# Attention backward on one core: loads of a head pair in one piece, taken in turn with the group's, and a tail that finishes each tile one step later

## The chip, the cores and the metric

The kernel runs on one core of a Trainium2 chip. A time is the device time of one execution in microseconds (us), and less is better. A core has five engines that run side by side and wait for each other by semaphores: TensorE (PE in the profile), VectorE (DVE), ScalarE (ACT), GpSimd (POOL) and SyncE (SP), which here does nothing but issue DMAs. Each engine takes its instructions strictly in the order of the program, and so a DMA that SP or POOL issues goes out only when everything ahead of it on that engine has gone out.

## The reference, cut to what matters

The kernel computes a transformer block, attention and a gated feed-forward side by side on one layer norm, and all its gradients:

```
xn  = layernorm(x)                          # x: 2048 rows of 448
out = x + attention(xn, wqkv, wo) + (silu(xn @ w_gate) * (xn @ w_up)) @ w_down
returns out and the gradients of x, wqkv, wo, w_gate, w_up, w_down for grad_out
```

Attention has 16 heads of 28 columns (padded to 32) over 2048 positions. With P = softmax(q k' / sqrt(28)) the backward pass needs dV = P' dO, dS = P * (dO V' - delta), dQ = dS K and dK = dS' Q. The gradient of x is the layer norm's backward of the sum of what comes back through wqkv, w_gate and w_up, plus grad_out.

## The kernel before, in words

The work has four stages, one after the other.

**Prologue and stage A** (0 to 657 us). Layer norm, the projection of q, k and v, attention forward, and the feed-forward with its weight gradients. Heads are taken in 4 groups of 4; a group's q, k and v, transposed, are tiles of 128 partitions (4 heads by 32) by 2048 positions. `proj_done` (L198) has POOL write them to DRAM (`vT_d`, `qT_d`, `kT_d`, one store each, L204 to L206), and `o_items` has POOL write the transposed gradient of the attention output there in four quarters (`dOT_d`, L525).

**Stage B** (657 to 1471 us), attention backward, lines 826 to 918. Heads go by pairs: 8 pairs, two to a group. A pair's work is 64 units, one for each 512 keys (kc), half of the queries (w) and 128 queries (qi), 512 units in all. In a unit PE forms the scores (L852) and dO V' (L863), both as products over 32 rows: the tile named qT holds q' of the two heads in its rows 0 to 63 and dO' in rows 64 to 127, and the tile named kT holds k' and v' likewise. ACT takes the exponential (L870), DVE multiplies to dS (tile `ds`, L881, 8 buffers), PE accumulates dV and dK from both (L749). dQ needs dS transposed: of 8 units two are transposed by PE (L776) and six by a DMA transpose that SP issues (`dsT`, L883). I call 8 units a **window** and number it W, 0 to 63. Beside this, a window has PE do one "job" of plain matrix products: a tile of rows of the output, of the gradient through the feed-forward, or a part of the wqkv gradient (L672 to L734). What a job needs (`ck`, 448 or 576 KB) SP loads two windows ahead (`job_load`, L655).

SP's order is written out by hand. In a window it issues at position 0 the job's load, at position 4 the loads of operands for what is to come, and at each of six units the transpose of `ds`; also every second window the transpose of a finished dK/dV block (`dkv_sp`, L762), and in the first two windows of a pair that of the last pair's dQ (`dq_sp`, L818). The loads to come wait in three lists: `pload` (the next pair's qT and kT), `gload` (the next group's row-major q, k, dO: `v_sp`, `vT`, `O_sp`) and `wload` (weights). `load_pair` (L546) makes the pair's loads from four DRAM tensors, since two of them go to rows 0 to 63 and two to rows 64 to 127; cut in two along the positions this gives 8 DMAs of 64 partitions by 1024 columns, 128 KB each. `load_group` (L558) makes 6 DMAs of 128 partitions by 1024 columns, 256 KB each. At position 4 up to two of `pload`, one of `gload` and two of `wload` are issued (L844):

```
for lst, n in ((pload, 2), (gload, 1), (wload, 2)):
    for f in lst[:n]:
        f()
    del lst[:n]
```

A pair's loads are so issued in the first four windows of the pair before it, and a group's in the first six windows of the group before it.

**Between** (1471 to 1494 us): the last part of the wqkv gradient.

**The tail** (1494 to 1548 us), lines 950 to 981: the gradient of x, 16 tiles of 128 rows. For a tile PE sums 14 products into PSUM (L957, L959); ACT copies it with a row sum s1 (`g_sb`, L963); DVE multiplies it by xn with a row sum s2 (`junk`, L966) and makes two numbers per row of s1 and s2 (`bb` L970, `cc` L972); ACT scales (`t1`, L975, which needs `bb`); DVE adds (`t2`, L977, which needs `t1` and `cc`); POOL adds grad_out (`dx`, L980); SP stores (L981). PSUM has 3 buffers for the tiles, the small tiles 3 each.

Of the kernel before, what the change touches and what calls it, by code (L numbers as in the profile page):

```python
# [10 lines left out]
ALU = mybir.AluOpType  # L11
# [26 lines left out]
def kernel(  # L38
# [27 lines left out]
    qT_d = dram.tile([G, P, S], BF16, name="qT_d")  # L66
    kT_d = dram.tile([G, P, S], BF16, name="kT_d")
    vT_d = dram.tile([G, P, S], BF16, name="vT_d")
    dOT_d = dram.tile([G, P, S], BF16, name="dOT_d")
# [128 lines left out]
    def proj_done(g):  # L198

        qT, kT, vT = (qk_tiles[(g, i)] for i in range(3))  # L200
        if g > 0:
            v = v_tiles[g] = qkp.tile([P, NT, P], BF16, name="v_sp")
            sp.dma_start_transpose(out=v[:], in_=vT[:])
        pool.dma_start(out=vT_d[g], in_=vT[:])  # L204
        pool.dma_start(out=qT_d[g], in_=qT[:])
        pool.dma_start(out=kT_d[g], in_=kT[:])  # L206
# [260 lines left out]
    def o_items(g, qc, o_ps):  # L467
# [29 lines left out]
        def do(i):  # L497
# [27 lines left out]
            pool.dma_start(out=dOT_d[g, :, qc * 512:(qc + 1) * 512], in_=dT[:])  # L525
# [20 lines left out]
    def load_pair(pr, parts):  # L546

        g, r = pr // 2, 64 * (pr % 2)
        q = qkp.tile([P, S], BF16, name="qT")
        k = qkp.tile([P, S], BF16, name="kT")  # L550
        qd[pr] = (q, k)
        n = S // parts
        return [lambda i=i, dst=dst, r0=r0, src=src: sp.dma_start(
                    out=dst[r0:r0 + 64, i:i + n], in_=src[g, r:r + 64, i:i + n])
                for r0, srcs in ((0, (qT_d, kT_d)), (64, (dOT_d, vT_d)))
                for dst, src in zip((q, k), srcs) for i in range(0, S, n)]
# [274 lines left out]
    for k in range(N + 2 * UW):  # L831
        W, pos = k // UW, k % UW
        if k < N:
# [7 lines left out]
            if pos == 4:  # L841
                if W == len(jobs) - 1:
                    wload.extend(load_w("wq", 2))
                for lst, n in ((pload, 2), (gload, 1), (wload, 2)):  # L844
                    for f in lst[:n]:
                        f()
                    del lst[:n]
# [74 lines left out]
    with ExitStack() as fin:  # L922
# [26 lines left out]
        wq = wtile["wq"]  # L949
        for t in range(NT):  # L950
# [7 lines left out]
            for n in range(3 * G):  # L958
# [17 lines left out]
            t2 = wk.tile([P, D], FP32, name="t2")  # L976
            dve.scalar_tensor_tensor(out=t2[:], in0=xn_sp[:, t, :D], scalar=cc[:, 0:1], in1=t1[:],  # L977
                                     op0=ALU.mult, op1=ALU.add)
            dx = wk.tile([P, D], BF16, name="dx")
            pool.tensor_tensor(out=dx[:], in0=t2[:], in1=dy_t[:, t, :], op=ALU.add)  # L980
            sp.dma_start(out=out1_d[:, t, :], in_=dx[:])  # L981
# [31 lines left out]
```

## Time and profile before

| | |
|---|---|
| time, median of 3 runs | 1550.76 us (1550.44 to 1550.81) |
| the profiled execution's own time | 1549.43 us |
| its span (first to last instruction) | 1547.7 us |
| PE, ACT, DVE, POOL busy over the span | 91%, 77%, 71%, 26% |
| stage A, 50 to 657 us | PE busy 573.2 of 607.0 us, DMA share 0.78 |
| stage B, 657 to 1471 us | PE busy 744.2 of 814.0 us, DMA share 1.07 |
| tail, 1494.3 to 1547.7 us | PE busy 43.0 of 53.4 us |

A line of the profile names the line of the kernel, the engine, the operation, and the tiles it writes and reads (out<-in). In a list in order of time the first two numbers are the start and the duration in us; "x3" means that three are merged into one line, and what stands in brackets is the idle time before them and what ended it. SPq and ACTq are the issuing of DMAs by SP and ACT. A table by stretches gives, for each stretch, its length and the busy time of each engine, then PEclk, the clock that TensorE was granted as a share of full speed, then the mean share of time that the 16 DMA engines were busy (packets that overlap count twice, so it can pass 1), and GB/s.

### The profile page before, as it was taken

The page shows a single profiled execution, that of the slowest core. Times are in us where ns is not written, and L with a number is a line of the kernel's source. Part 1 is how long each engine was busy: PE and PEld are TensorE (multiplying, and loading weights), DVE is VectorE, ACT ScalarE, POOL GpSimd, SP SyncE. Part 2 cuts the span into 40 slices and gives each one's busy share as a digit, 9 for nine tenths or more (in the row PEclk, how much of TensorE's full clock was granted, in tenths as well). Part 3 has the DMA queues.
Part 4 walks back from the last instruction along what each step waited for, and adds up shares of the span by engine and source line. Part 5 has one row for each costly group of instructions (what it writes and reads, how often), then busy time and mean ns, then how long its engine had stood idle before and what let it go on. Part 6 is the DMA issues. An engine that isn't in the chain of part 4 may idle for free.

```text
span 1547.7 us, 32024 instructions
## 1 busy us (share of the span) xinstructions
PE 1412.8 (91%) x12176; PEld 597.7 (39%) x12176; DVE 1099.4 (71%) x1421; ACT 1187.9 (77%) x1333; POOL 396.1 (26%) x664
## 2 busy tenths in 40 slices
PE   6899999999999989988988988989999889999987
PEld 3333333333333333433433444433335333543353
DVE  7654555656666657476877877878878789888935
ACT  6898988888788878676767867878778778888724
POOL 4341433343435355310110111111102101111033
PEclk9999999999999999999999999999999999999999
DMA  9985758767978689799999999999999999999994
GB/s 225 189 174 113 157 101 173 161 142 141 179 154 164 148 173 215 159 205 200 214 204 206 196 199 205 198 200 198 207 197 197 200 192 197 174 192 215 188 274 142
DMA packets 682106, 285.12 MB, mean 184 GB/s; under 512 B 637136, under 2 KB 650464, under 8 KB 681952
## 3 DMA queue, kind: packets, MB, share of 16 engines
q1 hardware_dynamic: 652016, 210.03, 74.6%
q0 software_dynamic: 25968, 64.53, 16.8%
q10 hardware_dynamic: 3968, 8.52, 1.6%
q8 instruction: 95, 1.56, 0.4%
q14 instruction: 59, 0.48, 0.1%
HBM read 67.34 MB, written 63.44 MB: 85 GB/s over the span
## 4 chain that ended last, share of the span: by engine, by line
PE 56%; DMA 13%; ACT 13%; DVE 8%; issue 6%; SPq 1%; POOL 1%; ACTq 0%; DVEq 0%; POOLq 0%
DMA dsT<-ds 9%; PE f_ps L357 7%; PE sd L852 6%; PE s_ps L600 6%; PE f_ps L383 6%; ACT E L870 5%; PE aux L719 4%; PE acc L749 4%; PE aux L796 4%; PE aux L776 4%; PE o_ps L582 4%; ACT eT L605 4%; DVE ds L881 3%; ACT dsT L783 3%; PE aux L713 3%
## 5 line engine op out<-in xcount | busy, mean ns | idle before, releaser
L881 DVE TENSOR_TENSOR ds<-sd,E 128x1024 bf16<-128x1024 f32 x512 | 611.4, 1220 | 137.5 <-DMA dsT<-ds 52.6
L870 ACT ACTIVATE E<-sd 128x1024 bf16<-128x1024 f32 x512 | 516.9, 1024 | 178.4 <-PE sd L863 140.2
L605 ACT ACTIVATE eT<-s_ps 128x1024 bf16<-128x1024 f32 x512 | 495.8, 1026 | 93.1 <-PE s_ps L600 89.6
L852 PE MATMUL sd<-kT,qT 32*128 32x512 bf16 x1024 | 201.8, 390 | 24.7 <-DVE ds L881 22.3
L863 PE MATMUL sd<-kT,qT 32*128 32x512 bf16 x1024 | 202.6, 389 | 23.6 <-ACT E L870 22.7
L749 PE MATMUL acc<-ds,v_sp 128*32 128x512 bf16 x1024 | 204.6, 395 | 0.7 <-DVE ds L881 0.7
L749 PE MATMUL acc<-E,O_sp 128*32 128x512 bf16 x1024 | 204.3, 395 | 0.2 <-ACT dkv_o L755 0.2
L600 PE MATMUL s_ps<-qT,kT 32*128 32x512 bf16 x1024 | 148.0, 386 | 7.8 <-ACT eT L605 5.6
L422 POOL DMA_DIRECT2D hd_d<-fT x168 | 126.9, 769 | 15.5 <-DVE fT L407 6.8
L383 PE MATMUL f_ps<-xnT,wgu 128*128 128x512 bf16 x448 | 118.8, 383 | 4.9 <-DVE w_sb L409 4.7
L764 POOL DMA_DIRECT2D dqkv_d<-dkv_o x64 | 39.3, 619 | 289.1 <-ACT dkv_o L755 287.3
L719 PE MATMUL aux<-W,ck 128*128 128x448 bf16 x448 | 108.4, 359 | 3.4
L852 PEld LDWEIGHTS <-qT 32*128 32x128 bf16 x1024 | 51.3, 91 | 154.1 <-issue 145.5
L582 PE MATMUL o_ps<-eT,v_sp 128*32 128x512 bf16 x1024 | 103.4, 394 | 0.6
L357 PE MATMUL f_ps<-xn_sp,f_sp 128*128 128x448 bf16 x448 | 99.1, 354 | 0.0
L749 PEld LDWEIGHTS <-O_sp 128*32 128x32 bf16 x1024 | 50.4, 94 | 113.4 <-issue 103.4
L600 PEld LDWEIGHTS <-kT 32*128 32x128 bf16 x1024 | 40.7, 91 | 137.7 <-issue 132.7
L776 PE MATMUL aux<-ident_bf,ds 128*128 128x128 bf16 x1024 | 79.4, 221 | 11.2 <-DVE dq_acc L808 5.8
L863 PEld LDWEIGHTS <-qT 32*128 32x128 bf16 x1024 | 65.4, 91 | 62.1 <-issue 58.2
L357 PEld LDWEIGHTS <-f_sp 128*128 128x128 bf16 x672 | 58.2, 98 | 77.4 <-issue 23.4
L776 PEld LDWEIGHTS <-ds 128*128 128x128 bf16 x1024 | 61.8, 98 | 39.8 <-issue 39.4
L395 DVE SCALAR_TENSOR_TENSOR g<-t_sb,f_ps 128x512 f32<-128x512 f32 x56 | 38.4, 686 | 53.3 <-ACT t_sb L393 53.2
(133 smaller groups left out, 1766.5 us busy)
## 6 DMA issues: line engine op xcount, KB each, us to landing
hd_d<-fT POOLq DMA_DIRECT2D x168, 128.0 KB, 4.4
ck<-hd_d SPq DMA_DIRECT2D x32, 448.0 KB, 4.4
ck<-hd_d SPq DMA_DIRECT2D x16, 576.0 KB, 5.1
dsT<-ds SPq DMA_TRANSPOSE x384, 4.2
dqkv_d<-dkv_o POOLq DMA_DIRECT2D x64, 64.0 KB, 3.8
dq_c<-dqkv_d ACTq DMA_DIRECT2D x5, 768.0 KB, 6.5
W<-wT_d SPq DMA_DIRECT2D x14, 224.0 KB, 3.6
out_dram<-dw_o POOLq DMA_DIRECT2D x28, 96.0 KB, 4.0
```

The source lines that it names most:

```text
L357: pe.matmul(acc[:, :D], lhsT=src[:, 12 * (t // 4) + 4 * wi + t % 4, :], rhs=rhs[:, t, :D], start=(t == 0), stop=(t == NT - 1))
L383: pe.matmul(st[name][:], lhsT=w(c), rhs=src[:, tsl, c, :], start=(c == 0), stop=(c == 3))
L582: pe.matmul(o_ps[HP * hh:HP * (hh + 1), :], lhsT=v[:, kt, HP * hh:HP * (hh + 1)], rhs=e[hh // 2][:, hh % 2, :], start=(kt == 0), stop=(kt ...
L600: pe.matmul(s_ps[:, j, :], lhsT=kT[r:r + HP, kt * P:(kt + 1) * P], rhs=qT[r:r + HP, qc * 512:(qc + 1) * 512], start=True, stop=True, tile_ ...
L605: act.activation(out=e[:], in_=s_ps[:], func=ACT.Exp, scale=SCALE)
L719: return [lambda n=n: pe.matmul(ps[:, :D], lhsT=t[:, n, :], rhs=w[:, n, :], start=(n == 0), stop=(n == NFC - 1)) for n in range(NFC)]
L749: pe.matmul(acc[r:r + HP, :], lhsT=src[:, qt, 64 * hp + HP * j:64 * hp + HP * j + HP], rhs=m[:, j, :], start=(qt == 0), stop=(qt == NT - 1 ...
L776: pe.transpose(ps[:, i, :], ds[:, i // 4, (i % 4) * P:(i % 4 + 1) * P], ident_bf[:])
L852: pe.matmul(s_ps[:, j, :], lhsT=q[HP * j:HP * j + HP, qt * P:(qt + 1) * P], rhs=kv[HP * j:HP * j + HP, kc * 512:(kc + 1) * 512], start=Tru ...
L863: pe.matmul(d_ps[:, j, :], lhsT=q[r:r + HP, qt * P:(qt + 1) * P], rhs=kv[r:r + HP, kc * 512:(kc + 1) * 512], start=True, stop=True, tile_p ...
L870: act.activation(out=E[k][:], in_=s_ps[:], func=ACT.Exp, scale=SCALE)
L881: dve.tensor_tensor(out=DS[k - 1][:], in0=d_ps[:], in1=E[k - 1][:], op=ALU.mult)
```

## The change

Three things are changed.

1. **One tensor for each operand of a pair.** `qT_d` and `dOT_d` become `qdo_d`, and `kT_d` and `vT_d` become `kv_d`: a slab for each pair whose rows 0 to 63 and 64 to 127 are what the pair's tile holds. `load_pair` loads a whole tile of 128 partitions at a time, so a pair has 4 loads of 256 KB instead of 8 of 128 KB, ordered first halves first. In exchange POOL's stores are cut by head pair: six of 64 partitions for three of 128 in `proj_done`, two for one in `o_items`.
2. **One load in a window.** In a window with an even number one piece of `pload` is issued, in one with an odd number one of `gload`; `wload` stays at two. A pair's four loads go out in windows 0, 2, 4 and 6 of the pair before, a group's six in windows 1, 3, 5, 7, 9 and 11 of the group before.
3. **The tail in two steps.** `t2`, `dx` and the store of tile t are issued after `bb` and `cc` of tile t+1, and `dx` of the last three tiles is made by DVE instead of POOL.

```diff
-    qT_d = dram.tile([G, P, S], BF16, name="qT_d")
-    kT_d = dram.tile([G, P, S], BF16, name="kT_d")
-    vT_d = dram.tile([G, P, S], BF16, name="vT_d")
-    dOT_d = dram.tile([G, P, S], BF16, name="dOT_d")
+    qdo_d = dram.tile([2 * G, P, S], BF16, name="qdo_d")
+    kv_d = dram.tile([2 * G, P, S], BF16, name="kv_d")
...
-        pool.dma_start(out=vT_d[g], in_=vT[:])
-        pool.dma_start(out=qT_d[g], in_=qT[:])
-        pool.dma_start(out=kT_d[g], in_=kT[:])
+        for hp in range(2):
+            rows = slice(64 * hp, 64 * hp + 64)
+            for dst, src in ((kv_d[2 * g + hp, 64:], vT), (qdo_d[2 * g + hp, :64], qT), (kv_d[2 * g + hp, :64], kT)):
+                pool.dma_start(out=dst, in_=src[rows, :])
...
-            pool.dma_start(out=dOT_d[g, :, qc * 512:(qc + 1) * 512], in_=dT[:])
+            for hp in range(2):
+                pool.dma_start(out=qdo_d[2 * g + hp, 64:, qc * 512:(qc + 1) * 512],
+                               in_=dT[64 * hp:64 * hp + 64, :])
...
-        g, r = pr // 2, 64 * (pr % 2)
...
-        return [lambda i=i, dst=dst, r0=r0, src=src: sp.dma_start(
-                    out=dst[r0:r0 + 64, i:i + n], in_=src[g, r:r + 64, i:i + n])
-                for r0, srcs in ((0, (qT_d, kT_d)), (64, (dOT_d, vT_d)))
-                for dst, src in zip((q, k), srcs) for i in range(0, S, n)]
+        return [lambda i=i, dst=dst, src=src: sp.dma_start(out=dst[:, i:i + n], in_=src[pr, :, i:i + n])
+                for i in range(0, S, n) for dst, src in ((q, qdo_d), (k, kv_d))]
...
-                for lst, n in ((pload, 2), (gload, 1), (wload, 2)):
+                for lst, n in ((pload, 1 - W % 2), (gload, W % 2), (wload, 2)):
...
+        def finish(t, t1, cc):
+            t2 = wk.tile([P, D], FP32, name="t2")
+            dve.scalar_tensor_tensor(out=t2[:], in0=xn_sp[:, t, :D], scalar=cc[:, 0:1], in1=t1[:],
+                                     op0=ALU.mult, op1=ALU.add)
+            dx = wk.tile([P, D], BF16, name="dx")
+            add = pool if t < NT - 3 else dve
+            add.tensor_tensor(out=dx[:], in0=t2[:], in1=dy_t[:, t, :], op=ALU.add)
+            sp.dma_start(out=out1_d[:, t, :], in_=dx[:])
+
         for t in range(NT):
...
             act.activation(out=t1[:], in_=g_ps, func=ACT.Identity, scale=rstd[:, t:t + 1], bias=bb[:, 0:1])
-            t2 = wk.tile([P, D], FP32, name="t2")
...
+            if t > 0:
+                finish(t - 1, *held)
+            held = (t1, cc)
+        finish(NT - 1, *held)
```

More of the change, by code (lines that the diff above doesn't have):

```diff
@@ L975 @@
             act.activation(out=t1[:], in_=g_ps, func=ACT.Identity, scale=rstd[:, t:t + 1], bias=bb[:, 0:1])
-            t2 = wk.tile([P, D], FP32, name="t2")
[L977 to L981, printed above, removed]
+            if t > 0:
+                finish(t - 1, *held)
+            held = (t1, cc)
+        finish(NT - 1, *held)
     cst.close()
```

## The prediction

> **What bounds the kernel now.** I read the span in slices first, then the waits, then the table by stretches for stage B, then SP's and DVE's instructions in order of time.
>
> ```profile
> PE   6899999999999989988988988989999889999987
> ...
> DMA  9985758767978689799999999999999999999994
> ```
>
> PE is nearly full everywhere, so gains lie only where it is held up. In stage B (slices 18 to 38) the DMA engines are full as well. The waits name what holds it up there:
>
> ```profile
> DVE ds L881 <- DMA dsT<-ds: 52.6, 38, 3.5
> ```
>
> In 38 cases, 52.6 us together, DVE has no free buffer for the next dS, since the transposes of the eight before it are not done. To see where, I took the start of every eighth exponential (ACT L870) and so the length of each window W. Windows in which SP loads no operands take 11.78 and 12.05 us in turn (12.51 on average in W1 to W16, whose jobs are larger). The long ones follow the loads. Over these floors: W2 to W5 10.1 us, W9 to W13 6.5, W18 5.2, W20 and W21 4.7, W26 to W28 5.1, W34 to W37 8.0, W42 to W45 5.8; together **45.4 us**. The table by stretches shows four windows without loads and then W35, W36 and W37:
>
> ```profile
> 1040.90:1088.50 47.60, 46.02 (x440) 19.40 (x440) 42.43 (x41) 39.07 (x43) 5.95 (x10) 1.00 1.10 199
> 1112.35:1128.40 16.05, 12.76 (x110) 5.13 (x110) 10.57 (x11) 9.40 (x12) 0.56 (x1) 0.89 0.98 199
> 1128.40:1142.10 13.70, 11.83 (x110) 4.85 (x110) 10.69 (x11) 10.17 (x12) 1.81 (x3) 0.96 1.12 211
> 1142.10:1156.00 13.90, 13.76 (x110) 5.25 (x110) 10.66 (x11) 9.56 (x11) 0.56 (x1) 0.79 1.06 181
> ```
>
> PE is 97% busy in the first row. In W35 it is not, and in W37 it is busy but at a clock of 0.79: the stall is paid a second time, in a slower clock after it. SP and DVE in W35:
>
> ```profile
> 1115.40 1.24 SPq L762 DMA_TRANSPOSE dkv_sp<-dkv_o  x1
> 1116.69 1.22 SPq L553 DMA_DIRECT2D qT<-dOT_d  x2
> 1117.95 1.59 SPq L564 DMA_DIRECT2D vT<-spk_d  x1
> 1119.64 4.00 SPq L883 DMA_TRANSPOSE dsT<-ds  x3
> ```
> ```profile
> 1115.81 3.49 DVE L881 TENSOR_TENSOR ds<-sd,E 128x1024 bf16<-128x1024 f32 x3 [2.54 <-DMA dsT<-ds]
> ```
>
> SP issues one DMA directly behind another, about 0.09 us apart. Three loads ahead of the transposes cost them 2.8 us here, while DVE waits for one. I measure SP's **lag**, from the end of a dS on DVE to the end of the issue of its transpose: 3.7 us at W24, then 6.6, 9.3 and 9.9 with two loads in each window; DVE waits begin near 10. From W29 to W32, with no loads, it falls from 5.5 to 4.1; from W45 to W48 from 7.5 to 3.8, and from W13 to W16 from 7.5 to 2.4. With 1.4 us of DVE's waits in those stretches taken off, that is 8.8 us in 9 windows: **SP has 0.98 us to spare in a window without loads.**
>
> The tail, one period:
>
> ```profile
> 1521.38 0.69 DVE L977 SCALAR_TENSOR_TENSOR t<-xn_sp,cc,t 128x448 f32<-128x448 bf16 x1 [0.85 <-ACT t L975]
> 1521.98 0.62 DVE L966 SCALAR_TENSOR_TENSOR junk<-sd,xn_sp 128x448 f32<-128x448 f32 x1
> 1522.52 0.09 DVE L966 DVE_READ_ACCUMULATOR junk<-sd,xn_sp 128x1 f32 x1
> 1522.52 0.67 DVE L970 SCALAR_TENSOR_TENSOR bb<-s,rstd 128x1 f32<-128x1 f32 x1
> 1523.12 0.15 DVE L972 SCALAR_TENSOR_TENSOR cc<-s,rstd 128x1 f32<-128x1 f32 x1
> 1524.11 0.69 DVE L977 SCALAR_TENSOR_TENSOR t<-xn_sp,cc,t 128x448 f32<-128x448 bf16 x1 [0.85 <-ACT t L975]
> ```
> ```profile
> 1522.15 1.03 POOL L980 TENSOR_TENSOR dx<-t,dy_t 128x448 bf16<-128x448 f32 x1 [1.70 <-DVE t L977]
> ```
>
> `bb`, one column wide, takes 0.67 us and ends when POOL's `dx` ends (1523.18); where POOL is idle it takes 0.16. Then DVE waits 0.85 for `t1`, which needs that `bb`. The period is 2.73 us; PE's 14 products take 2.65 (L957 starts 1494.10, 1496.75, 1499.40).
>
> **The change part by part.** Stage B, SP's side. A 64-partition load costs 0.53 + 0.09 to 0.59 + 0.09 us of issue; one of 128 partitions does too (`v_sp` 0.58), so I take 0.63 for the new qT loads. In the 16 windows of two pairs SP issues 8 + 8 + 6 = 22 loads now and 4 + 4 + 6 = 14 after. Three times (pair 1 to 6): 24 issues fewer, 15.1 us of SP. The rest is a matter of where: 14 x 0.63 = 8.8, with four `dq_sp` of 1.24 + 0.09 = 1.33, 5.3, makes 14.1 us, against 16 x 0.98 = 15.7 to spare. So the stage just fits, where it was packed into the first windows. What stays: the lag is already 8.5 and 10.1 at W0 and W1, before any load, so the first windows still stall (I take 3 us of 10.1); in W18 PE waits 3.6 us for `dq_sp`, issued in W17, and then loses 1.7 in half clock, of which a lag some 2 us less takes perhaps two fifths (3 us left of 5.2); and with a margin of 1.6 us in 16 windows I expect one stall with its slow clock for each group, 3 us each, 9. Of 45.4 us 15 stay: **gain 30.4 us**. The bounds: all of 45.4 gone, or only what the next paragraph leaves.
>
> The DMA queue's side. The loads carry the same bytes, in packets of 2048 bytes as before. The table above has 199 GB/s without loads and 211 in W36, so whether the queue has room is less clear than for SP. The Trainium skill, "DMA: Bandwidth & Descriptors", section "Issuing engines are not separate DMA queues", says that the time to issue is usually small against the DMA itself; by that rule it is bytes that count here and little is gained. The trace speaks against it in part: an issue of 0.58 us stands against the 256 KB that 206 GB/s carry in 1.27 us, so the issue is half of the transfer, not little.
>
> Loads later: a pair's last piece goes out at position 4 of its window 6, 12 units or 18 us ahead of its first use. A lag of 10 to 12.4 (the largest seen) and 3.7 us from issue to landing (`v_sp`) leave 2 us or more. Cost nothing, while the lag is at most 14.
>
> Stage A. POOL issues 12 + 16 = 28 stores more. A half store isn't in the trace; the whole ones take 0.53 to 0.58 us, `hd_d` of 128 KB 0.77. At 0.55 each, 15.4 us of POOL, which is busy 242 of 607 us there. Behind them stand POOL's `hd_d` stores, for which DVE waits three times (10.4 us, `fT`); between nothing and 15.4 I take **0.5 us**, near nothing, since those three are all the waits for POOL's stores that stage A shows on DVE. SP has two issues fewer there, which nobody waits for.
>
> Tail. `t2` of tile t now follows `cc` of tile t+1, so `t1` is ready, and POOL's `dx` of a tile is over before the next `bb`. DVE's and POOL's loop is then 0.69 + 0.08 + 1.03 + 0.16 = 1.96 us at its tightest, under PE's 2.65: PE sets the pace. PE's last tile ends at 1494.26 + 16 x 2.65 = 1536.7. Behind it: `g_sb` 0.64, `junk` 0.62, `bb` and `cc` 0.16, `t2` 0.69, `dx`, `t2` 0.69, `dx`. DVE's `dx` isn't in the trace: between `junk` 0.62 and POOL's 1.03; I take 0.69, that of `t2`, the same shape with two inputs in SBUF. Sum 4.18 and some 0.1 of gaps: 1541.0, against 1545.04 now. **Gain 4.0 us**; bounds 0 (if PE comes to wait for its loads, which it does not now) and 4.5.
>
> Sum: 1549.43 - 30.4 + 0.5 - 4.0 = 1515.5 for a profiled execution. The median lies 1.33 above the profiled one now; with that, **1517 us**.
>
> **The rivals.**
>
> *Bytes, not issues.* If the queue is full at 206 GB/s (W2 to W4 and W6 to W7 both show 205 to 206), 256 KB in a window of W0 to W15 cost 1.27 us wherever they stand; in later windows, which run at 199 without loads, some 90 KB find room and the rest costs 0.8. Each way 14 pieces in 16 windows: 17.8 + 22.4 = 40 of 45.4 us stay. Time 1549.43 - 5 + 0.5 - 4.0 + 1.3 = 1542. For it: the equal rates. Against it: from 1471 to 1494 us the core moves 259 GB/s, and W48 to W51, which load a pair but no `ck`, show no excess.
>
> *All of it.* No stall is left and the clock stays full: 1549.43 - 45.4 - 4.0 + 1.3 = 1501. Against it: the lag at W0.
>
> *Slower: the last piece comes late.* If SP's lag stays at its limit through the whole pair, because an even spread leaves it no window to recover, the piece issued in window 6 lands after the pair's first scores (L852) want it. It decides from a lag of 14.5 us at that point. The gain in stage B is then gone, and 7 pairs pay some 2 us and 1.7 us of slow clock each: 1550.8 + 26 - 4 = 1573. Against it: DVE's eight buffers stop the lag near 12.
>
> *It does not do what it says.* SP's transposes still come late for another reason, such as the long issues (1.8 to 2.4 us instead of 1.24) that recur without loads. Then the tail alone counts and the time is near that of the bytes.
>
> **How the numbers follow.** Forecast 62% (1505 to 1530), bytes or no effect 20% (1530 to 1547), all of it 9% (under 1505), slower 6%, no change 3%. The range for 8 in 10 is 1501 to 1541: it takes in the first, half of the third and most of the second. Under 0.2%, 3 us, this kernel's times can't be told from no change; faster 0.91, same 0.03, slower 0.06.
>
> **What would show it.** DVE's wait for `dsT` falls from 52.6 us to under 20; windows W2 to W45 come near 12.5 and 11.9 us; fewer stretches of stage B have a clock under 1; PE starts tail tiles 2.65 us apart throughout and `bb` takes 0.16. A stage B as long as before with evenly longer windows would show bytes; PE waiting at a pair's first L852 would show the late piece.

## The result and the profile after

The changed kernel takes **1535.66 us** (median of 5 runs, 1528.86 to 1545.24) against 1550.44 before (5 runs beside them, 1547.46 to 1550.81); the ratio is 0.991, with a 95% interval of 0.9882 to 0.9938. It is faster by 14.8 us where 33.8 were forecast (1550.76 to 1517). The profiled execution of the changed kernel is the longest of its five, 1545.24 us with a span of 1543.4. (Two executions further on, one of e9_narrow at 2873 us and one of the kernel before beside e18_x_pool at 2641, stand apart from all others and are left out of medians and ratios.)

The busy shares in 40 slices, of the changed kernel's page:

```profile
PE   6799999999899989989998999989999899999988
...
DMA  9986758686988788889999999999999999999994
```

In stage B (slices 18 to 38) PE's row looks as it did. The wait that carried the prediction has hardly moved, 48.2 us in 43 cases for 52.6 in 38:

```profile
DVE ds L879 <- DMA dsT<-ds: 48.2, 43, 3.1
```

The first exponentials of windows 0 and 48 and the last of all cut stage B in two. The table by stretches, of before and then of the changed kernel:

```profile
656.91:1281.47 624.56, 563.58 (x5676) 245.88 (x5674) 505.15 (x477) 464.64 (x500) 78.58 (x165) 0.98 1.07 201
1281.47:1470.43 188.96, 180.15 (x1926) 81.90 (x1925) 168.81 (x159) 153.71 (x166) 27.39 (x62) 0.99 1.09 192
```
```profile
670.19:1279.69 609.50, 558.80 (x5676) 244.08 (x5674) 504.72 (x477) 464.51 (x500) 78.98 (x166) 0.98 1.09 207
1279.69:1468.49 188.80, 180.41 (x1930) 82.05 (x1929) 168.77 (x159) 153.59 (x166) 27.34 (x62) 0.99 1.05 189
```

Windows 0 to 47 are 15.1 us shorter: PE's idle time in them falls from 61.0 to 50.7 us and its busy time from 563.6 to 558.8. The rest of stage B, where the loads are over but for the last pair's, is as before. The longest windows now are W10, W11, W26, W35 and W42, 14.3 to 15.6 us. And stage A ends at 670.19 us instead of 656.91, so that 13.3 us are lost ahead of stage B in this execution. The same four rows as in the prediction, W29 to W32, then W35, W36 and W37:

```profile
1043.08:1090.74 47.66, 46.02 (x440) 19.40 (x440) 42.47 (x41) 39.05 (x44) 5.93 (x10) 1.00 1.12 205
1115.35:1130.40 15.05, 12.84 (x110) 4.60 (x110) 10.63 (x11) 9.45 (x12) 0.56 (x1) 0.89 1.05 208
1130.40:1142.41 12.01, 11.57 (x110) 4.85 (x110) 10.59 (x11) 10.10 (x12) 1.81 (x3) 1.00 1.10 194
1142.41:1154.19 11.78, 11.44 (x110) 4.85 (x110) 10.62 (x11) 9.42 (x11) 0.56 (x1) 1.00 1.03 198
```

W36 and W37 are at their floor now, and W29 to W32, which have two loads now, stay there; but W35 is 15.05 us long (16.05 before). SP there:

```profile
1117.06 1.24 SPq L760 DMA_TRANSPOSE dkv_sp<-dkv_o  x1
1118.35 0.57 SPq L553 DMA_DIRECT2D kT<-kv_d  x1
1119.01 4.98 SPq L881 DMA_TRANSPOSE dsT<-ds  x3
1124.08 0.53 SPq L665 DMA_DIRECT2D ck<-hd_d  x1
```

One load takes 0.57 us of issue, and then three transposes take 4.98 us, where three of 1.24 with 0.09 between take 3.90. This could be the bytes of the load; one place doesn't show it, since before three transposes took 4.00 behind three loads. e9 and e10 below test it. The tail, DVE and then PE:

```profile
1521.78 0.15 DVE L978 SCALAR_TENSOR_TENSOR bb<-s,rstd 128x1 f32<-128x1 f32 x1
1521.89 0.16 DVE L980 SCALAR_TENSOR_TENSOR cc<-s,rstd 128x1 f32<-128x1 f32 x1
1521.97 0.68 DVE L951 SCALAR_TENSOR_TENSOR t<-xn_sp,cc,t 128x448 f32<-128x448 bf16 x1
1523.88 0.62 DVE L974 SCALAR_TENSOR_TENSOR junk<-sd,xn_sp 128x448 f32<-128x448 f32 x1 [1.23 <-ACT g_sb L971]
```
```profile
1520.30 0.54 PE L965 MATMUL sd<-pab,ident_bf 128*128 128x448 bf16 x2
1520.68 2.43 PE L967 MATMUL sd<-W,dq_c 128*128 128x448 bf16 x12
1522.95 0.54 PE L965 MATMUL sd<-pab,ident_bf 128*128 128x448 bf16 x2
```

`bb` takes 0.15 us, DVE waits only for the copy of PE's sums, and PE starts a tile every 2.65 us.

### The profile page after: what moved, and what is told of

It reads as the page before. It is cut to its first block, busy times and chain, and to the rows that moved or that the text cites. A ratio compares the mean times of both kernels' runs of the same rounds, so it can differ in the third digit from the quotient of the medians.

```text
span 1543.4 us, 32028 instructions
## 1 busy us (share of the span) xinstructions
PE 1414.6 (92%) x12176; PEld 598.3 (39%) x12176; DVE 1093.5 (71%) x1424; ACT 1188.8 (77%) x1333; POOL 407.6 (26%) x689
## 4 chain that ended last, share of the span: by engine, by line
PE 60%; DMA 13%; ACT 13%; DVE 7%; issue 6%; POOL 0%; SPq 0%; DVEq 0%; ACTq 0%; POOLq 0%
DMA dsT<-ds 8%; PE f_ps L356 7%; PE f_ps L382 6%; PE s_ps L598 6%; PE sd L850 6%; ACT E L868 5%; PE aux L717 5%; PE acc L747 4%; ACT eT L603 4%; PE o_ps L580 4%; PE aux L774 3%; PE aux L711 3%; PE aux L794 3%; DVE ds L879 3%; ACT dsT L781 3%
## 5 line engine op out<-in xcount | busy, mean ns | idle before, releaser
L879 DVE TENSOR_TENSOR ds<-sd,E 128x1024 bf16<-128x1024 f32 x512 | 610.8, 1218 | 123.4 <-DMA dsT<-ds 48.2
L850 PE MATMUL sd<-kT,qT 32*128 32x512 bf16 x1024 | 200.9, 389 | 18.4 <-DVE ds L879 16.2
L850 PEld LDWEIGHTS <-qT 32*128 32x128 bf16 x1024 | 50.9, 91 | 146.8 <-issue 138.2
L774 PE MATMUL aux<-ident_bf,ds 128*128 128x128 bf16 x1024 | 79.7, 221 | 10.7 <-DVE dq_acc L809 5.2
```

Source lines behind the costliest of these rows:

```text
L774: pe.transpose(ps[:, i, :], ds[:, i // 4, (i % 4) * P:(i % 4 + 1) * P], ident_bf[:])
L850: pe.matmul(s_ps[:, j, :], lhsT=q[HP * j:HP * j + HP, qt * P:(qt + 1) * P], rhs=kv[HP * j:HP * j + HP, kc * 512:(kc + 1) * 512], start=Tru ...
L879: dve.tensor_tensor(out=DS[k - 1][:], in0=d_ps[:], in1=E[k - 1][:], op=ALU.mult)
```

## The experiments

Two things are worked out for each kernel from the trace of its profiled execution: where stage B begins ("A to") and how long it is, from the first to the last of its exponentials; and, for windows 0 to 47, their length and for how much of it SP is issuing: the sum of its DMA instructions with 0.09 us between two. "Loads" counts the loads of pairs and groups that SP issues in it, and "transposes" is the time of the issues of `dsT`, some 285 in every kernel. One kernel's executions lie up to 20 us apart (e8; those of before run from 1541 to 1559 us in these batches), so that a stage's length in one profile is good to some us only. How good, eight kernels show that issue the same in stage B (changed, e4, e7, e12, e14 to e17): B is 790.3 to 800.0 us, on average 796.0, W0-47 601.5 to 609.6, and the transposes take 440.6 to 451.5, on average 446.2. The changed kernel's own transposes are the longest of the eight. The ratio is to runs of the kernel before on the same chip, with its 95% interval.

| kernel | median us | ratio | A to | B | W0-47 | SP issuing | loads | transposes |
|---|---|---|---|---|---|---|---|---|
| before | 1550.44 | | 656.9 | 813.5 | 624.6 | 614.3 | 66 | 443.6 |
| changed | 1535.66 | 0.991 (0.9882-0.9938) | 670.2 | 798.3 | 609.5 | 601.1 | 42 | 451.5 |
| e1_turns | 1548.91 | 1.0003 (0.9985-1.002) | 660.9 | 813.5 | 624.4 | 617.2 | 66 | 447.3 |
| e2_layout | 1543.91 | 0.9947 (0.9925-0.9969) | 662.3 | 795.1 | 604.3 | 595.4 | 42 | 448.8 |
| e3_tail | 1545.29 | 0.9974 (0.9955-0.9994) | 657.9 | 811.3 | 623.4 | 615.9 | 66 | 447.2 |
| e4_whole_stores | 1529.31 | 0.9866 (0.9839-0.9892) | 657.2 | 790.3 | 601.5 | 591.2 | 42 | 440.6 |
| e5_big | 1538.04 | 0.9924 (0.9897-0.995) | 663.7 | 797.8 | 609.9 | 598.4 | 21 | 461.1 |
| e6_pool_loads | 1543.99 | 0.9975 (0.9953-0.9997) | 661.8 | 803.9 | 615.1 | 595.0 | 0 | 470.4 |
| e7_late_stores | 1552.83 | 1.0014 (0.9994-1.0034) | 679.7 | 793.5 | 605.5 | 597.5 | 42 | 446.6 |
| e8_pool_halves | 1552.49 | 1.0019 (0.9993-1.0044) | 662.7 | 824.0 | 634.2 | 612.4 | 0 | 482.0 |
| e9_narrow | 1524.49 | 0.9834 (0.9798-0.987) | 668.5 | 784.3 | 596.4 | 587.2 | 42 | 436.6 |
| e10_no_loads | 1508.93 | 0.9735 (0.9705-0.9765) | 663.9 | 768.5 | 579.5 | 554.8 | 0 | 435.1 |
| e11_uncut | 1541.52 | 0.995 (0.9927-0.9973) | 659.3 | 806.9 | 617.9 | 603.7 | 42 | 453.2 |
| e12_one_store | 1562.85 | 1.0093 (1.0059-1.0127) | 680.0 | 800.0 | 609.1 | 598.1 | 42 | 447.2 |
| e13_two_block_loads | 1657.19 | 1.0703 (1.0673-1.0733) | 679.4 | 902.4 | 699.0 | 688.9 | 42 | 541.7 |
| e14_do_cut | 1530.04 | 0.9877 (0.9852-0.9901) | 655.1 | 795.7 | 605.0 | 594.8 | 42 | 444.3 |
| e15_qkv_cut | 1534.38 | 0.9913 (0.9887-0.994) | 659.4 | 796.2 | 605.1 | 595.9 | 42 | 445.6 |
| e16_sp_stores | 1535.03 | 0.9889 (0.9864-0.9914) | 660.3 | 798.4 | 609.6 | 600.1 | 42 | 448.5 |
| e17_act_stores | 1572.76 | 1.013 (1.0103-1.0157) | 703.8 | 795.9 | 606.9 | 598.3 | 42 | 445.4 |
| e18_x_pool | 1527.39 | 0.9859 (0.9826-0.9891) | 663.4 | 789.5 | 600.6 | 589.4 | 42 | 447.8 |

The two columns W0-47 and SP issuing are the main finding: wherever SP issues loads, they differ by 7 to 14 us in some 600. **SP issues for about 98% of these windows, before and after.** The price of one issue isn't fixed: of the changed kernel's 286 transposes 143 are issued in under 1.3 us and the longest takes 4.46, and in e10, which has no such loads, it is 164 of 286 and 4.03. What holds a long issue is not shown.

### Each part alone

**e1_turns**, part 2 alone, with two 64-row pieces in an even window:

```diff
-                for lst, n in ((pload, 2), (gload, 1), (wload, 2)):
+                for lst, n in ((pload, 2 * (1 - W % 2)), (gload, W % 2), (wload, 2)):
```

> Part 2 alone: the kernel before with its 8 loads of 64 partitions for a pair, two of them in each window with an even number, and a piece of the group's in each with an odd one. Stage A and the tail are as before. The bytes of stage B stand in the same windows as in the changed kernel, but SP issues 22 loads in 16 windows, not 14. Theory SP (what holds stage B up is SP's time to issue): 24 issues more than in the changed kernel, 15 us of SP, so at most a third of the changed kernel's gain in stage B of 15 us: 1545 to 1550 us. Rival, bursts (what counts is how many bytes stand in a window, however many issues carry them): the whole 15 us, 1534 to 1537 us. Either way stage A is as long as before (first exponential of stage B near 657 us).

Stage B is 813.5 us as before, to the tenth, and the ratio is 1.0003. To spread the loads gains nothing.

**e2_layout**, part 1 alone: the changed kernel's DRAM layout, stores and `load_pair`, with before's windows (one of `pload`, one of `gload`) and tail:

```diff
-                for lst, n in ((pload, 2), (gload, 1), (wload, 2)):
+                for lst, n in ((pload, 1), (gload, 1), (wload, 2)):
```

> Part 1 alone: one tensor for each operand of a pair and whole-tile loads, but in the windows in which the kernel before issues the same bytes (one of 256 KB for two of 128 KB, and one piece of the group, in each of the first windows of a pair). The tail is as before. Theory SP: 28 issues fewer, stage B 10 to 15 us shorter. Rival, bursts: stage B as before, 813 us. Stage A has the split stores: if they cost what the profile of the changed kernel shows (13 us), its first exponential of stage B comes at 665 to 672 us; if that was an accident of one execution, near 657. Sum by theory SP with dear stores 1543 to 1552 us, by bursts with dear stores 1555 to 1563, by bursts with stores for nothing 1550.

Stage B is 795.1 us: all of the change's gain there comes with the 24 loads fewer in windows 0 to 47, whatever windows they stand in.

**e3_tail**, part 3 alone: `finish` and `held` as in the change's diff, all else as before.

> Part 3 alone: only the tail in two steps. Both theories: PE sets the pace of 2.65 us, the tail is 4.0 us shorter, 1546 to 1547 us, and stages A and B as before. If the gain seen in the profile hangs on what stage B leaves, less.

From the first product of the tail to the end it is 49.2 us (53.6 before, 49.6 in the changed kernel), and the median is 4.4 us under before's 1549.74 of that batch. The tail's term stands.

### What a load costs in stage B

**e5_big**, the changed kernel with the loads whole:

```diff
-                pload.extend(load_pair(pr + 1, 2))
+                pload.extend(load_pair(pr + 1, 1))
...
-                gload.extend(load_group(pr // 2 + 1, 2, vp if pr // 2 % 2 else ksp))
+                gload.extend(load_group(pr // 2 + 1, 1, vp if pr // 2 % 2 else ksp))
```

> The changed kernel with whole loads instead of halves: a pair's two tiles by 2 DMAs of 512 KB and a group's by 3 of 512 KB, so 7 loads in 16 windows instead of 14 (and 22 before), with the same bytes. Theory SP, with the 0.8 us for a load that the first four experiments give (stage B excess 45 us with 22 loads in 16 windows, 22 to 29 with 14): 21 loads fewer, 13 to 17 us off stage B, 1519 to 1523 us. Rival, bytes (a load costs what its bytes take from the transposes behind it in the queue, and the loads of 64 partitions were dear for another reason): no gain, 1534 to 1537, or a loss, since one load of 512 KB now stands ahead of a transpose for twice as long.

No gain in stage B (797.8), though 21 issues are gone. The loads' issues, with 0.09 each, fall from 31.0 to 15.0 us, but the transposes take 461.1 instead of 451.5 and SP's other DMAs 87.3 instead of 83.6: 13.3 of the 16.0 us are taken back. The 461.1 lie clear of the 440.6 to 451.5 above; the 3.7 us of the other DMAs do not stand out.

**e6_pool_loads**, the changed kernel, and **e8_pool_halves**, before's layout and windows with the tail in two steps: `load_pair` and `load_group` for later pairs and groups issue by POOL.

```diff
-        return [lambda i=i, dst=dst, src=src: sp.dma_start(out=dst[:, i:i + n], in_=src[pr, :, i:i + n])
+        return [lambda i=i, dst=dst, src=src: (eng or sp).dma_start(out=dst[:, i:i + n], in_=src[pr, :, i:i + n])
...
-                pload.extend(load_pair(pr + 1, 2))
+                pload.extend(load_pair(pr + 1, 2, pool))
```

> The changed kernel with the pair's and the group's loads of stage B issued by POOL, which is busy for 106 of 814 us there, instead of SP; the same loads, bytes and windows. Theory SP: SP has no load left but weights, the excess of stage B over its floors falls from 22 to 29 us to under 8, 1512 to 1520 us. Rival, bytes: the transposes share the 16 DMA engines with these bytes whoever issues them, stage B as in the changed kernel (790 to 798 us), 1533 to 1537.

> The kernel before, with its whole stores, its 8 loads of 64 partitions for a pair and its windows, but these loads and the group's issued by POOL, and with the tail in two steps. Theory SP: neither the number nor the shape of the loads matters once SP does not issue them: stage A as before (657 to 661 us), stage B under 780 us instead of 813, tail 49.6, together 1500 to 1510 us. Rival, bytes, and shape: stage B as before, since the same bytes stand in the same windows, 1545 us.

Both lose: 1543.99 us against the changed kernel's 1535.66, and 1552.49 against 1545.29 for e3, which differs from e8 in the loads' engine alone. SP issues no load, and yet its transposes take 470.4 and 482.0 us. In e6's W10 and W11, where two loads of POOL's (issued at 791.79 and 793.95) fall together with `ck`, three transposes take 11.31 us:

```profile
791.73 1.03 SPq L659 DMA_DIRECT2D ck<-hd_d  x1
792.86 0.39 SPq L661 DMA_DIRECT2D x_c<-in_A_x_dram  x1
793.68 11.31 SPq L881 DMA_TRANSPOSE dsT<-ds  x3
```

So with no load on SP the transposes' issues are longer, not shorter. That the second queue lets the loads' bytes collide with the transposes, where SP's order had kept them behind one another, fits both runs but was not tried by itself. They spoke against a theory of issues alone; the next two part the terms.

**e9_narrow** and **e10_no_loads**:

```diff
     def load_pair(pr, parts):
+        if pr > 0:
+            qd[pr] = qd[0]
+            return [lambda j=j: sp.dma_start(out=scr[:], in_=qdo_d[pr, :, j * 64:j * 64 + 64]) for j in range(4)]
...
     def load_group(g, parts, kpool):
+        if g > 0:
+            spt[g] = spt[0]
+            return [lambda j=j: sp.dma_start(out=scr[:], in_=spq_d[g, :, j * 64:j * 64 + 64]) for j in range(6)]
```

In e10 both return an empty list.

> The changed kernel with the loads of stage B's windows cut to 64 columns (16 KB instead of 256 KB) into a tile that nobody reads; the operands of the first pair and group are used for all pairs, so the computed values are not the reference's. It issues as many DMAs on SP as the changed kernel does, in the same places, and leaves the bytes out. If the issues on SP are the price of a load, stage B stays within 5 us of the changed kernel's 798.3. If the bytes are (their time on the DMA engines that the transposes share), stage B falls by 15 to 25 us, to 773 to 783, and the excess of the windows in the first 48 from 28.9 to under 12. If neither is, since the residue is made by other DMAs (the chunk loads, dkv_sp's transposes, code fetches), it falls by 5 to 12.

> As the one with the narrow loads, but the loads are left out altogether (the values are again not the reference's). Beside it this prices the issue alone: by the issue theory stage B falls by 20 us or more against the changed kernel (30 issues in the first 48 windows at 0.6 to 0.8 us are 18 to 24 us), nearly all of it between the narrow loads and this; by the theory of the bytes it is at most 5 us below the narrow loads. What is left of the excess then belongs to no load.

(The loads in windows 0 to 47 are 42, not 30, and 46 in all.) Both theories held half: without the bytes stage B falls by 14.0 us, just under what the theory of the bytes asked for, and without the issues by another 15.8. Against the average of 796.0 us above the bytes are 11.7, and by the ratios the two steps are some 12 and 15. The bytes show in the transposes (436.6 us, under all eight of 440.6 to 451.5), the rest in SP's own issues. Without loads DVE's wait is nearly gone and PE is busy 96% of windows 0 to 47; here is the wait and the stretch in e10:

```profile
DVE ds L885 <- DMA dsT<-ds: 3.7, 4, 1.4
```
```profile
663.88:1243.35 579.47, 555.90 (x5676) 247.16 (x5674) 506.38 (x477) 464.16 (x500) 78.99 (x166) 0.99 1.08 199
```

All 45 us of before (624.6 - 579.5) belong to the loads, and the DMA share is 1.07 to 1.09 with or without them: that column could not have told it.

**e11_uncut**, the kernel before with 64-row loads of all 2048 columns:

```diff
-                pload.extend(load_pair(pr + 1, 2))
+                pload.extend(load_pair(pr + 1, 1))
...
-                for lst, n in ((pload, 2), (gload, 1), (wload, 2)):
+                for lst, n in ((pload, 1), (gload, 1), (wload, 2)):
```

> The kernel before with the pair's eight loads of 64 rows by 1024 columns (128 KB) made four of 64 rows by 2048 (256 KB), one per window instead of two: as many bytes per window as before, and as many issues as the changed kernel, but still 64 rows each. If the number of issues or packets' order matters, stage B falls from 813.5 to 795 to 800; if it is the half width (64 rows instead of 128 go to fewer DMA engines or take them for longer), it stays at 809 to 814 and the median within 3 us of before.

It lies between: stage B falls by 6.6 us. SP's issues are as few as in the changed kernel, but the transposes are 9.6 us longer than before (6.0 longer than in e3), as they are longer in e5, the other kernel whose packets have 4096 bytes instead of 2048 (in the trace 278 and 229 ns each on average, against 115 before and 125 in the changed kernel). That it is the packet's length which holds the transposes up is a guess from these two and was not tried by itself; `ck` comes in packets of 3584 and 4608 bytes in every kernel.

**e18_x_pool**, made last, on e16 (below): the `x_c` loads go from SP to POOL.

```diff
-            sp.dma_start(out=x[:], in_=x_d[:, j[1], :])
+            pool.dma_start(out=x[:], in_=x_d[:, j[1], :])
```

> The changed kernel with the half stores of q, k and v on SP (1535.0 us, stage B 798.4), and with the 16 loads of x rows for the output's tiles (112 KB each, windows 0 to 15) issued by POOL instead of SP (outputs as the reference's). SP issues 6.9 us for these 16, and 1.4 between them. If SP's own time is what windows 0 to 47 last (601 of 610 us in the changed kernel, 614 of 625 before), each issue taken away pays: windows 0 to 15 shorten by 6 to 9 us, stage B to 789 to 793, the median to 1526 to 1530. If bytes or collisions with a second queue set it, as with the pair's and group's loads on POOL, stage B is 797 to 803 and the median 1534 to 1538.

SP issues 10.7 us less than in e16, windows 0 to 47 are 9.0 shorter, and the median of 1527.39 us is the lowest of the kernels that compute the reference, below both before and the changed kernel (the ratio's interval, up to 0.9891, just overlaps the changed kernel's, from 0.9882). The place was not as expected: windows 0 to 15, where the 16 loads stood, give 2.9 of the 9.0 us, and 16 to 47 the rest, more than a lag can carry over. That part may be chance: kernels with one and the same stage B differ by 8 us in these windows.

### What the stores cost in stage A

**e4_whole_stores**, the changed kernel with before's four DRAM tensors and whole stores; loads of 128 rows from them:

```diff
+        return [lambda i=i, dst=dst, src=src: sp.dma_start(out=dst[:, i:i + n], in_=src[pr // 2, :, i:i + n])
+                for i in range(0, S, n) for dst, src in ((q, (qT_d, dOT_d)[pr % 2]), (k, (kT_d, vT_d)[pr % 2]))]
```

> The changed kernel with the stores of stage A whole again, as in the kernel before: three of 128 partitions in proj_done, one in o_items. To keep the loads as in the changed kernel (4 of 128 partitions and 256 KB for a pair, in turn), a pair's tiles are loaded from a group's whole tiles, so that the operands of attention backward are wrong ones and the gradients with them; sizes and instructions are the same. Theory (the 28 stores more hold stage A up): stage A as before, first exponential of stage B near 657 us, stage B as in the changed kernel, 1528 to 1533 us. Rival (the 13 us of stage A were an accident of that execution): a time like the changed kernel's, 1534 to 1537 us, with a stage A that is now and then longer.

The median is 6.4 us below the changed kernel's. In the profiles stage B begins at 659.2 us on average where stores are whole (before, e1, e3, e4, e8, e11: 656.9 to 662.7) and at 665.1 where they are cut (changed, e2, e5, e6, e9, e10: 661.8 to 670.2). The 28 further stores cost some 6 us.

**e14_do_cut** and **e15_qkv_cut** are e4 with one kind of store cut in two:

```diff
+            for hp in range(2):
+                pool.dma_start(out=dOT_d[g, 64 * hp:64 * hp + 64, qc * 512:(qc + 1) * 512],
+                               in_=dT[64 * hp:64 * hp + 64, :])
```
```diff
+            for dst, src in ((vT_d, vT), (qT_d, qT), (kT_d, kT)):
+                pool.dma_start(out=dst[g, rows], in_=src[rows, :])
```

> The kernel with whole stores of wrong operand rows (it left 1529.3 us, stage A 657.2; outputs of the backward part not the reference's), with only the 16 stores of dO cut in two of 64 rows each. If these 16 make stage A longer, it comes to 661 to 666 us and the median to 1533 to 1536; if the 12 of q, k and v do, both stay where they were, at 657 to 660 and 1528 to 1531.

> The same kernel with only the 12 stores of q, k and v cut in two of 64 rows each. By the first theory (dO) nothing moves, 657 to 660 and 1528 to 1531; by the second, that 512 KB in two DMAs land later and hold the ring of POOL's queue for the hidden layer's stores, stage A is 661 to 668 and the median 1533 to 1537. The rival to both is that the number of stores does it, wherever they stand: then each of the two kernels shows about half, 2 to 4 us.

The medians are 0.7 and 5.1 us above e4's: the 12 further stores of q, k and v cost it, the 16 of dO do not. (In e15's profile stage A is only 2.2 us longer; the medians carry this.)

The traces show where most of it is lost: in the first group, behind the first stores of q, k and v. From the first to the 33rd of the 512 exponentials of stage A (`eT`) the six kernels with whole stores take 36.2 to 39.7 us, 37.8 on average, and the six with cut ones 40.3 to 45.6, 42.3 on average: 4.5 of the 5.9 us by which the two averages of stage A differ. There PE waits for `dyT`, the transposed grad_out that SP makes by DMA while POOL's stores go out. In the changed kernel it is

```profile
PE f_ps L382 <- DMA dyT<-dy_sp: 2.9, 1, 2.9
```

and in the other five with cut stores 2.9 to 8.6 us, in e15 3.4, in e14 1.3, with whole stores at most 0.4. The issue of SP's last transpose of `dyT` there takes 7.0 to 9.0 us with whole stores (6.96 before), 8.2 to 12.0 with cut ones (8.99 in the changed kernel), and 2.0 in e7, e16 and e18, where the stores of q, k and v don't stand on POOL at that time.

**e7_late_stores** moves the six stores of q, k and v from `proj_done` to the head of `sp_layouts`.

> The changed kernel with the stores of q, k and v taken out of proj_done and put at the head of sp_layouts, one quarter of a group later; for the first group this is at 70 us, after the prologue, not at 32 us. Theory (the split stores of the first group hold back the transposes of dy, dyT, for which PE waits near 55 us): steps 8 to 16 of stage A come back from 23 to 24 us to 19 to 20, so 3 to 4 us less than the changed kernel, 1531 to 1533 us. Rival (the loss is in POOL's queue all along stage A, where hd_d stores come later behind the new ones): less than 1 us, 1535.

Neither came: stage A ends at 679.7 and the median is 1552.83. The theory's part is there, no wait for `dyT` is left and the 33 exponentials take 35.1 us, but more is lost later. DVE waits for the hidden layer's stores behind them in POOL's queue, in e7 and then in the changed kernel:

```profile
DVE fT L407 <- DMA hd_d<-fT: 26.0, 3, 16.2
```
```profile
DVE fT L406 <- DMA hd_d<-fT: 12.7, 2, 7.0
```

**e16_sp_stores** and **e17_act_stores** take them out of POOL's queue:

```diff
-                pool.dma_start(out=dst, in_=src[rows, :])
+                sp.dma_start(out=dst, in_=src[rows, :])
```

(`act` in e17.)

> The changed kernel with its 24 half stores of q, k and v issued by SP instead of POOL (outputs as the reference's). If these stores cost stage A their 5 us because they stand in POOL's queue ahead of the hidden layer's stores (hd_d), stage A comes to 657 to 661 us and the median to 1529 to 1533, as with whole stores. If it is their bytes on the DMA engines, or if SP's transposes stand behind them instead, stage A stays at 662 to 672 and the median at 1534 to 1542.

> The same 24 half stores issued by ACT. By the theory of POOL's queue stage A comes to 657 to 661 us and the median to 1529 to 1533; against it stands that 24 issues of some 0.6 us lie on ACT ahead of its exps (14 us; ACT is busy for some 80% of stage A, so that about 3 us of it would show): then 660 to 665 and 1532 to 1538. If ACT waits for the last k tile with exps behind it, stage A is 670 or more.

On SP stage A ends at 660.3 us, as the theory of POOL's queue expected, but at 663.4 in e18, whose stage A is the same, and the median of 1535.03 is in the other theory's range (before's was 1553.71 in this batch, some 4 us above the other batches): not settled. The wait for `dyT` is gone, yet the 33 exponentials take 40.6 us in e16; DVE there waits 5.0 for `f_sp`, which SP also transposes, behind its stores. On ACT it is much worse, 703.8 us: the issues of six in a row grow from 0.47 to 2.40 us, and the next exponential of stage A stands behind them.

```profile
143.59 0.47 ACTq L205 DMA_DIRECT2D kv_d<-vT  x1
144.10 0.61 ACTq L205 DMA_DIRECT2D qdo_d<-qT  x1
144.75 0.94 ACTq L205 DMA_DIRECT2D kv_d<-kT  x1
145.73 2.40 ACTq L205 DMA_DIRECT2D kv_d<-vT  x1
148.17 2.28 ACTq L205 DMA_DIRECT2D qdo_d<-qT  x1
150.49 1.90 ACTq L205 DMA_DIRECT2D kv_d<-kT  x1
152.49 1.02 ACT L603 ACTIVATE eT<-s_ps 128x1024 bf16<-128x1024 f32 x1 [7.36 <-DMA kv_d<-kT]
```

**e12_one_store** and **e13_two_block_loads** try to have both, whole stores and loads of 128 rows, with one DMA over two blocks of 64 rows, on the store's side and on the load's:

```diff
+            pool.dma_start(out=qdo_d[2 * g:2 * g + 2, 64:, qc * 512:(qc + 1) * 512], in_=dT[:])
```
```diff
+    qdo_d = dram.tile([2, G * P, S], BF16, name="qdo_d")
...
+        return [lambda i=i, dst=dst, src=src: sp.dma_start(out=dst[:, i:i + n], in_=src[:, 64 * pr:64 * pr + 64, i:i + n])
```

> The changed kernel, with the same layout in DRAM and the same loads, but each transposed operand goes out in one store again: its 128 rows are written to the two pairs' halves by one DMA with a destination of two blocks of 64 rows (12 + 16 stores less on POOL; outputs as the reference's). If the cut stores are what made stage A longer, stage A goes back to 657 to 659 us (670.2 in the changed kernel's profile), stage B stays at 790 to 799, the tail at 49.6, and the median falls to 1527 to 1532, as with the whole stores of wrong rows (1529.3). The rival: that run gained from where its rows lay in DRAM, or stage A differs by chance; then stage A stays at 664 to 671 and the median at 1534 to 1538.

> The changed kernel with the block moved from the store to the load: q and dO of all heads lie one behind the other (2 x 512 rows), so that every store is whole (12 + 16 stores less on POOL), and a load of SP takes two blocks of 64 rows at once into 128 partitions (outputs as the reference's; the same number of loads, of the same bytes). If the cut stores cost stage A its 6 us, stage A comes to 657 to 661 us; if a load of two blocks is as cheap on SP's queue as one of 128 rows, stage B stays at 790 to 800, and the median is 1527 to 1532, the version that beats both. The rival: two blocks are as dear here as in the stores (1562.9 with stores of two blocks), or as loads of 64 rows; then stage B is 805 or more and the median 1540 or more.

In e12 neither side had it: stage A ends at 680.0 us and the median is 1562.85, far over both ranges; PE waits 11.6 us for `dyT`. In e13 the rival won by far, with a stage B of 902.4 us and a median of 1657.19. The issue of such a load is cheap (0.53 us), but the three transposes behind it take 10.31 us:

```profile
781.97 0.53 SPq L550 DMA_DIRECT2D kT<-kv_d  x1
782.59 10.31 SPq L878 DMA_TRANSPOSE dsT<-ds  x3
```

In the trace the 128 packets of 2048 bytes of such a load take 6.19 us from first to last, at 97 ns each (medians over windows 0 to 47): 128 x 0.097 / 6.19 = 2.0 are in flight at a time. In the changed kernel it is 1.70 us at 120 ns, so 9.0. (Stage A holds the first pair's two loads of this form, 512 KB each, so its 679.4 us say nothing on the stores; its first 33 exponentials, with whole stores, take 38.6.) The Trainium skill, "DMA: Bandwidth & Descriptors", section "Why a DMA increments its semaphore by 16 and not by 1", says that the number of DMA engines that share a transfer is the largest up to 16 which divides the slowest dimension of both access patterns; for two blocks that is 2, and the trace agrees, 2.0 in flight. Which engines took them it does not show.

## Why the prediction was right or wrong

**The step that failed** is "SP has 0.98 us to spare in a window without loads" and what was made of it, "14.1 us against 15.7 to spare. So the stage just fits". The gain in stage B was put at 30.4 us and is 15.2 (813.5 to 798.3): of the 45.4 us 15 were to stay, and 30.0 stay (609.5 to e10's 579.5 in windows 0 to 47). The prediction's own numbers could have shown it: by the same budget the kernel before needs 22 x 0.63 + 5.3 = 19.2 us of SP in 16 windows and has 15.7, so it should stall for 3.5 us in 16 windows or 10.5 in 48. Even if the spare is counted only in the 10 of 16 windows that hold loads, 9.8 us, it comes to 9.4 or 28; the page shows 45.4. So neither the spare nor the place of the loads could explain the stall. The traces give the terms, for windows 0 to 47:

- The spare. Without any load SP is idle for 579.5 - 554.8 = 24.7 us (e10); the budget had 3 x (15.7 - 5.3) = 31.2.
- An issue. A load takes 0.65 us on SP and 0.09 between (43.3 / 66 before, 27.2 / 42 in the changed kernel), 0.74 instead of 0.63: issues of 1 us and more are among them.
- The bytes. Beside the loads the transposes take 443.6 us before and 451.5 in the changed kernel, against 435.1 without: 8.5 and 16.4 us that the budget did not have (5.5 to 16.4 over the eight kernels with the changed kernel's stage B).
- The rest. SP idles for 10.3 us before and 8.4 in the changed kernel, time that no kernel here put to use: in none whose loads SP issues is it under 7.

Added up (an account of the time, not a test), before: 66 x 0.74 + 8.5 - 24.7 + 10.3 = 43, near the 45.1 by which it is longer than e10; the changed kernel: 42 x 0.74 + 16.4 - 24.7 + 8.4 = 31, near 30.0. The windows without loads had not been idle before: SP caught up in them what it lagged from the others. A load moved there takes away the catching up; that the sum is zero is what e1 shows.

**The term of issues was right in size, partly by luck.** "24 issues fewer, 15.1 us of SP": SP issues 13.2 us less and windows 0 to 47 are 15.1 shorter; e2 shows that it needs no other part of the change. It is less a pure price of issues than it looks: in these two profiles the loads' own issues fell by 24 x 0.74 = 17.8, the transposes gave back 7.9, and SP's other DMAs took 2.9 less, and the last two are within what one kernel's profiles differ by. The average of 796.0 us makes the gain in stage B 17.5.

**The rival of bytes** came nearer in time (1542 us), but in part by luck: its gain of 5 us in stage B is a third of the 15.2, and the loss in stage A, which it did not have, made up for much of that. Its mechanism holds half: 12 to 14 us of the loads' price are bytes, but they show as longer issues of the transposes on SP, not as a full rate of the DMA engines, which show the same share without the loads. The Trainium skill, "DMA: Bandwidth & Descriptors", section "Issuing engines are not separate DMA queues", says that DMAs of all issuing engines run on the same DMA engines, and that the time to issue is usually small against the DMA itself. The runs fit the first, since loads moved to POOL's queue gained nothing (e6, e8), and not the second: 46 issues cost 15.8 us of stage B (e9 to e10). The Trainium skill, "DMA: Bandwidth & Descriptors", section "Rules for kernel authors", says to use one transfer of 128 partitions instead of two to disjoint halves of the partitions. e2 bears this out: 813.5 to 795.1 us.

**Stage A** was put at +0.5 us and costs some 6 by the medians of e4 and the changed kernel, and 13.3 in the one profile. The bound of 15.4 held it; the value was taken at the wrong end, because POOL was priced by the waits for its `hd_d` stores alone. Those hardly grew (`fT`, 10.4 to 12.7 us); most of the loss stands where PE waits for `dyT`, which SP transposes beside the cut stores of q, k and v (e15), and that wait is not in the prediction. Why cutting these stores holds the transposes longer is open, and so is the rest of the loss: taken off POOL's queue the stores ended that wait and left the median the same.

**The tail** was right: 53.6 to 49.6 us, a period of 2.65, `bb` at 0.15, `dx` on DVE at 0.62 for the 0.69 that was taken. The **late last piece** did not come: no wait of PE at L850 in the changed kernel is for a DMA. Of **it does not do what it says** the forecast, the tail's gain alone, did not come, since stage B is shorter; its condition did in part, since the transposes still come late (DVE's wait 48.2 of 52.6 us) and long issues recur without loads (up to 4.03 us in e10).

Of the gain of 33.8 us that was forecast 19.0 are missing in the medians: by the stages 15.2 in stage B and 5.5 in stage A, 1.7 more than are missing, which the spread of the runs leaves open.

## What to carry to other kernels

Before loads are moved to where a queue "has room", add up the whole time that the issuing engine spends issuing in that stage and divide it by the stage: at 98% fewer issues helped here (e2), and another order did not (e1). Test a budget of spare time on the kernel before first: if it does not give the stall that is there, it is wrong. To lay out DRAM so that one load fills 128 partitions paid on the queue that was full, but the stores that had to be cut for it had a price of their own, some 6 us, and not in a wait for the stores themselves: look also at the transposes that run beside them.

## What the runs showed of the hardware

- A DMA whose access pattern has two blocks as its outer dimension ran with 2.0 packets in flight instead of 9.0, and made this kernel 7% slower with 28 such loads of 256 KB in stage B and two of 512 KB before it.
- A store of two blocks on POOL's queue takes 22 to 26 us to land, and each of two of half the size 7.4 to 9.5; in one block the same 512 KB took 6.3 to 9.1 in the kernel before. The rows are e12's, then the changed kernel's:

```profile
kv_d<-vT POOLq DMA_DIRECT2D x4, 512.0 KB, 22.1
qdo_d<-qT POOLq DMA_DIRECT2D x4, 512.0 KB, 25.3
```
```profile
kv_d<-vT POOLq DMA_DIRECT2D x8, 256.0 KB, 7.4
qdo_d<-qT POOLq DMA_DIRECT2D x8, 256.0 KB, 9.2
```

- Such stores also add packets of 4 bytes: POOL's queue has 16368 ahead of 650 us in e12, 6128 in the changed kernel and 5840 before.
- The same issue on ACT took 0.47 us as the first of six in a row and 2.40 as the fourth.
